# Threshold attention and a three-way maxout FFN on one core: 23 of 288 half tiles masked by GpSimd, two maxout buffers for three, and a new written order

## The chip, the cores and the metric

One core of a Trainium2 chip runs the whole program. The metric is device microseconds of one execution; several executions of a kernel are timed and their median is given. The engines are TensorE (PE in the profile, with PEld for its weight loads), VectorE (DVE), ScalarE (ACT), GpSimd (POOL) and SyncE (SP, which only issues transfers here).

## The reference

Eight batches, eight heads, 576 tokens, head size 64; then a feed-forward block over 4608 tokens with 512 model and 768 hidden columns.

```python
scores = (q @ k.T) / sqrt(64)
scores = where(scores >= rowmax(scores) - tau, scores, -1e9)      # tau = 0.02
attn   = exp(scores - rowmax(scores));  attn /= attn.sum(-1) + 1e-9
x      = concat_heads(attn @ v)                                    # 4608 x 512
out    = maximum(maximum(x @ w1, x @ w2), x @ w3) @ w_out
```

So every score row needs its maximum, a mask (scores more than tau below the maximum count nothing), an exponential, a sum and a division.

## The kernel before, in words

**Tiling.** A tile of scores is 128 query rows by 2 x 576 keys; its two halves (128 x 576, one for each of two heads) are handled apart and are the unit of this text. There are 288 half tiles: 8 batches, 2 groups of four heads in each, 9 row blocks in a group, 2 halves. A half is computed into a PSUM bank pair `sc`; four such bank pairs (numbered 0 to 3) serve all products of TensorE, and each use of one must wait until the use before it has been read out.

**The passes over a half.** `maximum` (DVE) copies the negated scores from PSUM to an SBUF tile `z` (or to one of the two `stage` tiles) and takes their extreme `nm` on the way. After that the digit of the half in the table `MASKED` chooses:

- `0`: `threshold` (DVE, one column) makes `th` = -nm - tau; `exponents` (ACT) masks with a Prelu of slope 2^-100 on one side, and `numerators` (ACT) takes the exponential and the row sum. Two ACT passes, one DVE pass.
- `1`: `exponents` (ACT) takes the exponential; `numerators` (DVE) masks it by comparing with exp(-tau) and sums. One ACT pass, two DVE passes; the second reads `z` twice from SBUF.
- `2` and `3`: like `0` and `1`, but ACT reads the scores from PSUM.

Then `reciprocals` (DVE) gives `rs` for both halves, `normalized` (POOL) writes z times rs as the bf16 tile `P`, and `turned` (SP) issues the transposing transfer from `P` to `ptq`. `product` (TensorE) multiplies values by `ptq` into `o`, which ACT or DVE copies to `xt`.

**The FFN.** For each of six hidden blocks three products `ph` of `xt` with the three weights are formed. ACT copies the first to a tile `hm`, DVE takes the maximum of the second with `hm` in place, and of the third with `hm` into `hT`. Then `po` = hT times the output weights, copied out by ACT as `ob` and stored. The last batch is done in two parts (`SPLIT`).

**The order.** Nothing is scheduled by a program at run time: `ORDER` is a string in which each letter issues one step, and each engine runs its own steps strictly in that order. Capital letters are TensorE's (S scores, T transposes of q and k, O value product, F first half of an FFN product, B its second half, N a ninth chunk), with the bank pair behind most of them. Small letters: m `maximum`, s `threshold`, e `exponents`, k and n `numerators` (k on DVE, n on ACT), r `reciprocals`, p `normalized`, t `turned`, h the ACT copy to `hm`, v the DVE maxima, u the copies `ob`, a and c the copies of transposed q and k, q the swapped copies `qs` (mostly POOL), y and z casts on POOL, l and g loads. All steps are recorded under one line of a helper (L93 in the profile), so the tiles' names tell the groups apart.

Of the kernel before, what the change touches and what calls it, by code (L numbers as in the profile page):

```python
# [21 lines left out]
FLAT = 2.0 ** -100  # L22

MASKED = """
220202110002002100110000100020020312000112012010100000000010100000001100
001000111010000101100000000000110001100000011110110200100000100010000000
110001101110100100010000001001100100000100101111102300000100100000001000
001000110100100001000000000100100001011110100011011100002100001000001013
"""


# [2 lines left out]
ZBUFS = 9  # L34
MORE_Z = 72
PBUFS = 6

SPLIT = {7: ((0, 1), (2, 3, 4))}
# [3 lines left out]
ytS1erkpT2agmnT3pclesqS2aqetS0meqlrnspmS1eqsT2nmpS3tnrcS0zlemS2eprmS3npmtS0npsgS1sermpS2emyS3eptmT0eplmS1ayl  # L42
meS0kynS2tssT3snkynkercperlT3pmnpmntqremS0lasprgeT3pmeS2psstnplnS0mzecesqrmS3etqkeS2gpnmS1npsmtnS0prmleS3pmS
2npsmnS0yrsmetperS2epmO1eqtnkplemnzswT2teS3rplS1empnmS3tpnssrS1klepS0mapermtS2epmT1S3nmqtnkO2qemncpS3txrskT1
peS2rmeS0ptmegpamS2npS1ertsmpnlkzS2elmS3eS0mpnlO1srkepsmnO2tyeprgwnpmT1xS3cpeS0sszmF2eS1meBqkF0ngqT3shrsmBay
S2tvpnF3rpemS1BpemF0pnsvT2BnyctS1esrlsT2mphS3lezS1maF0myntpT2sS3ngrcqF1eBmpnS2svpBnrmS3peS0tmeyF2zmnF3lBsvep
S0rhkBptesF2mgeS1zvF0nsmBpteBsrgvpnF1kS3phS2semBnqmF0S3evqF2ntrmBpelS1spvBnlmS3qhF0rsmepS1tnBpsmS3ezvS2eS1rm
pF0etsyO3mnlkngpO2eswetkBxrmpT3nF2rvpaS1BnqmS0hspS3meF2prS1smntBzesmF3ezvT0tBeclT1yS2pnvS0apsmtS3eyrmlS1epS2
mepF0mnqsmnS3tkBnkeF1restpkumeS2prtBumlperkpS0ustS2umS3pesmS1eqtT0mO2nlpceqsrmO3ntywelkS0pxlS1meF3prnS2smBye
myF0thpskS1oeBpF2nlvF3nlrmBpeBkpS1hstsvS0eF3lrmpnF2mBepBsveF1nT0vBtarkS3lhqS2smleF0prF1mnBysntBveS2plvnS0pom  # L50
F3nyS1pmeBsysmF0thT2rrlpeS1clF3epsmBnqT2svBaS1evqS2nmF0pS3nmqBtnmT2pS1hrcpS3esmS0petF2melS1rmpBnF3skpetF0sve
BlBmnF2vhtF1esrBkpnS0vtT3npBmS2arvpS0ermO3eqtsmepT1swntpS0cF2epesmtnS3kT1nS0mtBessrkpameS3preS1mS0uqmuS3mpnS
1tsmS2pnoS0rempS3lempO1lnkqlemO2lnymeO0srkpetkeF3swxykxpT2BercnprtS1uyS2upmF0termqS3eBymN2lhsskpelkS0eF3ertm
S1pjBlmeS0plvF2npS1mnyF3tpmnBsopT0nvBaS1kF2ieqrssmS0hlpBmelT1qF3snrvF0epcBlepS2vBnpsmtS1nS3rmphS2mnpF1smeS0B
snmF3tevS2T0mF1atBrsekpBevS0thS2pmF3nymS1qeBrsmnpS0tvF2eplF1rmnpBskeBptF3hsvS0eBrsstpmnS1lvT2qeO0mpnlscnT3wS
1etF2srramS0lnqBmlF3eqvT1nBcpS0thF2pemS1perS3mpBnmS0ptesO1smpnkteF3yvxT0BraktyS2esS1vpeS0mpnS3meqF2mnyrmpnT0
S1lceBqmeptrskS0pulS3muS1epmS2teF0rmplnskpeS1mtO3eklekO2esrmpesBknpwxS1kutS2urmopS3nF0myeS1mBetpsmF2hlS3rkep
BlmnF0S1prnsvT3tepBmF2apsssvS1eBtqmeS0qrS3hmtS1epsmF2lnpF0mleF3koBnBrvpeBstyvS1phsS2nmF3emS0nrS1tpmBnprS2smn
F0pveF1pBsremT3ptevBpS2chF0tnmF3ekBT1nvS2aBsmlnF0qvS1eS2rtrespmS3eBmqF1hmpT2nBcpS3ekpT2O0sasvterlmpO2ekqntwS
3xklpS1eF2ssmnF0yrBnmyS3evBptemS1plhS2ssmT3eyF0rcpeF1mBpntT3vnByS2ravpS0nmtpS3nsmS1eF2srmpektepS3slmnS0Bmeqn  # L60
mT1ktuS3urS0lcpeO2rlmpelmpeO3klpelweF1kqnsxS0rkepS2tmS3eBymemepS0kuF3quT2smeBtrF1kphoS0aBmnpS3tsN2rnvplnmpS1
erkpF0tjsF3mnBpsseBvS2ihrS1pmelS0mqeF3S2mnytBpmnoS1rF0eprsvF2ntpmBeBvqF1htskpS3esS0rmetS2pnmF3pBnmF0pesvT2te
BcF1nsBrvpntBskphT2F3erS0vlapBmnF1qvS2etpBmT0hS3rscpnF2lmS1qesS0sempBemS3yF1nvtS0nmBnT2ssrmpO3etspveF0wnS1rk
BpaS3tmhS2elqsF1mlS0qnmS3ermpBF2espsmS0npvBeS3tmeS1rvpO0ntmnsmS2yxS3empF0eskyerT1mpeS2cBtnypsmelkS3ulS2muS1e
smT0O3nsrplnpO2awetmeF3rkpxseT0S1ycntS2meF0poBrnsmpnkpF1ukBurS2shBqemF3oepvS0lS2nsmqF1emBptBnvF0hrrS2speS3mp
F1emBpntT2vepF3BssaktS0nvlBemS2hS1rsmptF0nS3mpeBmtnT2F1svnF3cetBBsrnvpS2hsrqS0meS1pmeT3F2sprmaS0npBmeF3ptsvn
S1qS0mnBtqmeS2yF1prevS0epssBmnS3qmS2htpmF0nlF1keBsmBertvO3pnvepF0serwpT2nBcpF3hktS1eBsrsmpnT0S2vtpaS1remqT3S
0nmyF2qectT1BpasmS3epvS1nS0mqnF2rmpemtpT3eS1keqS0smBercntpS1mupS3emF0ukessS1rmtpnBmopkS2uskS1eO3rukekO0yxeO3
ynwtprmopS0xmpS2emF3peS1mteBrsmpS0nF2pmhtS1nkBS3evF0nstmN2erkpeF1mBjpsBevS2hskF0eF3rkpteBmF1nBpveBkO2hsrvpeS
0rtwS1pnmF2npmS3eBympF1ntrvS0epBmpS2rF3svtpeS0mnpS1sBmiF2smhF0ntkBBervpS1etF3smpnF2BervpS1hsBpnmF0tevS3F1nmB  # L70
etrBkpO2vhO3nspS1xrwepS0mpF3smS2etF1snmBeBstvnS2S0veS3meF1snkeF2rmpnmpeBnkBerrptukpuO3rN1xpuO0jpuO3wptF1xpF2
hF0tvF1vF3hF0vtF1vF2hF0viF1vF2ohF0voF1vF3hF2vF1vF3hF2vO1vO0wF2xF3F1huF0vF3vF2ohF1vF3vF2hF0vF1vF3hF0vF2vF3hF1
vF2vF0hF1vF2vF0uF1ouN0ofjdi
"""


# [28 lines left out]
def kernel(  # L105
# [273 lines left out]
    def exponents(c, r):  # L379
        z = c["z", r]  # L380
        src, sign = (c[r], -1.0) if direct(c, r) else (z, 1.0)
        if masked(c["g"], c["idx"], r):
            scalar.activation(out=z, in_=src, func=AF.Exp, bias=c["nm", r], scale=-sign)
        else:
            th = c["nm", r] if direct(c, r) else c["th", r]
            scalar.activation(out=z, in_=src, func=AF.Prelu, bias=th, scale=sign, alpha=FLAT)

    def numerators(c, r):
        z, acc = c["z", r], c["sm"][:, r:r + 1]
# [89 lines left out]
    def ffn(b, part):  # L479
# [219 lines left out]
    def flow(what, fn):  # L699
        while True:  # L700
# [7 lines left out]
    line = {k: [] for k in "menkrptahvuxwcqsjf"}  # L708
# [10 lines left out]
    def issue(what, where):  # L719
# [27 lines left out]
        elif what == "m":  # L747
            c, r = line["m"].pop(0)
            maximum(c, r)
            line["e"].append((c, r))  # L750
            if not masked(c["g"], c["idx"], r) and not direct(c, r):
                line["s"].append((c, r))
        elif what == "s":
            threshold(*line["s"].pop(0))
        elif what == "e":
            c, r = line["e"].pop(0)
            exponents(c, r)
            line["k" if masked(c["g"], c["idx"], r) else "n"].append((c, r))
        elif what in "nk":
            c, r = line[what].pop(0)  # L760
            if "sm" not in c:
                c["sm"] = small.tile([128, 2], F32, name="sm")
            else:
                c["summed"] = True
            numerators(c, r)
        elif what == "r":
            c = made[line["r"].append(0) or len(line["r"]) - 1]
# [62 lines left out]
```

## Time and profile before

| what | value |
|---|---|
| three runs | 444.09, 441.63 and 441.38 us, median 441.63 |
| span of the profiled execution | 440.2 us (1.43 us below the median of the runs) |
| TensorE, ScalarE, VectorE, GpSimd busy | 95%, 92%, 89%, 72% of the span |
| granted TensorE clock | 0.988 on average |

The profile is that of one execution, taken on the core itself; its span runs from the first to the last instruction, and the timed runs hold what lies around it too. An engine's busy time is the union of its instructions; two neighbouring instructions of one engine overlap a little, so the spacing of starts in the timeline is the price of one in a full queue, and the duration is somewhat more. A busy TensorE is modelled and is not TensorE at its peak.

### The profile page before, as it was taken

The page shows a single profiled execution, that of the slowest core. Times are in us where ns is not written, and L with a number is a line of the kernel's source. Part 1 is how long each engine was busy: PE and PEld are TensorE (multiplying, and loading weights), DVE is VectorE, ACT ScalarE, POOL GpSimd, SP SyncE. Part 2 cuts the span into 40 slices and gives each one's busy share as a digit, 9 for nine tenths or more (in the row PEclk, how much of TensorE's full clock was granted, in tenths as well). Part 3 has the DMA queues.
Part 4 walks back from the last instruction along what each step waited for, and adds up shares of the span by engine and source line. Part 5 has one row for each costly group of instructions (what it writes and reads, how often), then busy time and mean ns, then how long its engine had stood idle before and what let it go on. Part 6 is the DMA issues. An engine that isn't in the chain of part 4 may idle for free.

```text
span 440.2 us, 14283 instructions
## 1 busy us (share of the span) xinstructions
PE 418.9 (95%) x5188; PEld 313.6 (71%) x5190; DVE 393.9 (89%) x1248; ACT 403.6 (92%) x834; POOL 317.0 (72%) x420
## 2 busy tenths in 40 slices
PE   7696789999999999999999999999999999999996
PEld 6353446787788776787678777887688777786873
DVE  4888899999999999999999999999889999998542
ACT  4999999999999999999999999999999998989521
POOL 1988999998787778867786778886585776554400
PEclk9987999999999999999999999999999999999999
DMA  6999999999999999999999999999698778583812
GB/s 190 276 239 214 270 215 260 263 252 252 220 277 224 237 165 242 291 160 232 189 242 238 202 182 273 192 199 208 135 237 153 147 109 185 102 169 72 192 50 85
DMA packets 213959, 88.50 MB, mean 201 GB/s; under 512 B 189184, under 2 KB 202240, under 8 KB 213888
## 3 DMA queue, kind: packets, MB, share of 16 engines
q1 hardware_dynamic: 213360, 86.96, 95.4%
q8 instruction: 41, 0.67, 0.6%
q10 hardware_dynamic: 528, 0.62, 0.5%
q14 instruction: 30, 0.25, 0.2%
HBM read 35.65 MB, written 9.44 MB: 102 GB/s over the span
## 4 chain that ended last, share of the span: by engine, by line
PE 78%; DVE 5%; POOL 5%; issue 4%; ACT 3%; DMA 2%; SPq 1%; DVEq 0%; POOLq 0%; ACTq 0%
PE ph L93 31%; PE sc L93 26%; PE po L93 10%; PE o L93 8%; POOL P L93 4%; PE tp L93 3%; ACT z L93 3%; DVE z L93 3%; DMA qm<-in_q_dram 2%; SPq L93 1%; DVE kt L93 1%; POOL w L93 1%; DVE stage L93 0%; DVE hm L93 0%; POOL qs L93 0%
## 5 line engine op out<-in xcount | busy, mean ns | idle before, releaser
L93 POOL TENSOR_SCALAR P<-z,rs 128x576 bf16<-128x576 f32 x250 | 202.0, 819 | 59.1 <-DVE rs L93 30.4
L93 DVE TENSOR_SCALAR_CACHE_REDUCE z<-sc 128x576 f32<-128x576 f32 x250 | 183.2, 749 | 12.2 <-PE sc L93 8.1
L93 PE MATMUL sc<-kt,qs 64*128 64x256 f32 (+2 forms) x640 | 179.8, 417 | 5.5 <-DVE z L93 3.9
L93 PE MATMUL sc<-kt,qt 64*128 64x320 f32 (+2 forms) x640 | 180.9, 429 | 3.1 <-DVE z L93 1.2
L93 PE MATMUL ph<-xt,w 64*128 64x288 bf16 (+2 forms) x2160 | 172.0, 283 | 0.2 <-DVE hm L93 0.2
L93 PEld LDWEIGHTS <-w 64*128 64x128 bf16 (+1 forms) x2160 | 128.0, 94 | 31.6 <-issue 4.0
L93 ACT ACTIVATE z<-z,th 128x576 f32<-128x576 f32 x161 | 120.5, 767 | 2.2 <-DVE th L93 1.9
L93 ACT ACTIVATE z<-z 128x576 f32<-128x576 f32 x175 | 117.6, 674 | 0.2
L93 PEld LDWEIGHTS sc<-kt,qs 64*128 64x128 f32 (+1 forms) x640 | 92.4, 179 | 22.5 <-DVE z L93 8.6
L93 PEld LDWEIGHTS sc<-kt,qt 64*128 64x128 f32 (+1 forms) x640 | 92.0, 179 | 14.7 <-DVE z L93 3.5
L93 DVE SCALAR_TENSOR_TENSOR z<-z 128x576 f32<-128x576 f32 x75 | 61.7, 827 | 1.4 <-ACT z L93 1.1
L93 POOL COPY qs<-qt 64x640 f32<-64x640 f32 (+3 forms) x66 | 45.9, 695 | 19.5 <-ACT qt L93 16.1
L93 ACT ACTIVATE z<-z,nm 128x576 f32<-128x576 f32 x72 | 53.9, 767 | 0.0
L93 PE MATMUL po<-wo,hT 64*128 64x512 bf16 (+3 forms) x454 | 53.3, 354 | 0.3
L93 DVE TENSOR_TENSOR hm<-ph,hm 128x576 bf16<-128x576 f32 (+2 forms) x54 | 37.0, 685 | 9.8 <-PE ph L93 9.6
L93 ACT ACTIVATE hm<-ph 128x576 bf16<-128x576 f32 (+2 forms) x54 | 31.9, 590 | 14.3 <-PE ph L93 13.8
L93 PEld LDWEIGHTS <-hT 64*128 64x128 bf16 (+2 forms) x456 | 28.4, 95 | 18.5 <-issue 2.6
L93 DVE TENSOR_TENSOR hT<-ph,hm 128x576 bf16<-128x576 f32 (+2 forms) x54 | 36.9, 683 | 2.8 <-PE ph L93 1.0
L93 PE MATMUL o<-ptq,vb 128*64 128x512 bf16 (+2 forms) x544 | 38.7, 282 | 0.2 <-DVE z L93 0.2
L93 POOL TENSOR_SCALAR P<-stage,rs 128x576 bf16<-128x576 f32 x38 | 29.5, 783 | 11.7 <-DVE rs L93 8.4
L93 ACT ACTIVATION_READ_ACCUMULATOR z<-z 128x1 f32 x175 | 33.6, 192 | 0.0
L93 PEld LDWEIGHTS <-vb 128*64 128x64 bf16 x544 | 22.4, 111 | 14.0 <-issue 5.6
(44 smaller groups left out, 412.2 us busy)
## 6 DMA issues: line engine op xcount, KB each, us to landing
vm<-in_v_dram SPq DMA_DIRECT2D x32, 256.0 KB, 4.6
qm<-in_q_dram SPq DMA_DIRECT2D x15, 512.0 KB, 4.7
km<-in_k_dram SPq DMA_DIRECT2D x15, 512.0 KB, 5.4
out_dram<-ob SPq DMA_DIRECT2D x14, 512.0 KB, 4.5
stage<-in_moe_w_dram SPq DMA_DIRECT2D x9, 512.0 KB, 5.6
ptq<-P SPq DMA_TRANSPOSE x144, 4.5
vr<-in_v_dram SPq DMA_DIRECT2D x16, 128.0 KB, 3.8
stage<-in_moe_w_out_dram SPq DMA_DIRECT2D x3, 512.0 KB, 5.5
```

The source lines that it names most:

```text
L93: ins = fn(*a, **kw)
```

## The change

A new digit `4` in `MASKED` stands for 23 half tiles, the 83rd being the first and the 278th the last. For such a half `maximum` and `threshold` run as for `0`. Then GpSimd makes two passes: `marked` (letter b) computes (z + th) times 2^100 and writes it as int8 into the high byte of each element of a bf16 tile `far`, and `moved` (letter C) adds `far` to `z`. `exponents` (letter G) is then a single ACT pass, the exponential with the row sum. There is one `far` tile. The tiles `hm` go from three to two. The digits of other halves change as well: `0` from 187 to 173 halves, `1` from 84 to 78, `2` from 14 to 12, `3` from 3 to 2; the first 48 digits are as before. `ORDER` is a new string almost from its start, with the same steps in it otherwise.

```diff
+    def on_pool(c, r):
+        return by_mask[2 * number[c["g"], c["idx"]] + r] == "4"
     def exponents(c, r):
         z = c["z", r]
         src, sign = (c[r], -1.0) if direct(c, r) else (z, 1.0)
+        if on_pool(c, r):
+            scalar.activation(out=z, in_=z, func=AF.Exp, bias=c["nm", r], scale=-1.0, accum_out=summed(c)[:, r:r + 1])
+            return
...
+    far = [one.tile([128, S], BF16, name=f"far{x}") for x in range(FARS)]
+    for t in far:
+        vector.memset(t, 0.0)
+    def marked(c, r):
+        c["far", r] = t = far[next(fars) % FARS]
+        pool.tensor_scalar(out=t.bitcast(mybir.dt.int8).rearrange("p (n x) -> p n x", x=2)[:, :, 1],
+                           in0=c["z", r], scalar1=c["th", r], scalar2=FAR, op0=OP.add, op1=OP.mult)
+    def moved(c, r):
+        pool.tensor_tensor(out=c["z", r], in0=c["z", r], in1=c["far", r], op=OP.add)
...
-                    st["hm", f] = hp_.tile([128, nr, n], BF16, name="hm", bufs=3)
+                    st["hm", f] = hp_.tile([128, nr, n], BF16, name="hm", bufs=2)
...
-lllllllllT0laqqlcT1aS2lcqqgmS0S3lemS1lmnT2lmeS3lsaS0mnqlqemT3lyerclcapsnS1lS2eqmlS3qemznmS2perS1mnpsmnpT3ske
+llllllllllT0laT1qqlcagS2qqclS0mS3lmS1elmlT2nlmS3elsamS0lqnlT3qmeylrcecapS1snS2qmeS3qmzemnS2peS1rmptT3nsmpnsk
```

Three places show how the steps moved. On ScalarE, the steps ahead of its first copy `hm` (first batch; `z<-z,th` is the Prelu of a half, `z,sm<-z` the exponential with sum, `z<-z,nm` the exponential without). Before:

```order
L93 ACTIVATE xt<-o 128x576
L93 ACTIVATE z<-z,th 128x576 x3
L93 ACTIVATE z,sm<-z 128x576
L93 ACTIVATE hm<-ph 128x576
L93 ACTIVATE qt<-tp 128x2x320
```

and now:

```order
L95 ACTIVATE xt<-o 128x576
L95 ACTIVATE z<-z,th 128x576
L95 ACTIVATE z<-z,nm 128x576
L95 ACTIVATE z,sm<-z 128x576
L95 ACTIVATE hm<-ph 128x576
```

Four softmax passes stood between the last copy `xt` and the first `hm`, now three; over the whole list from the start there are 102 ACT steps ahead of the first `hm` before and 100 now.

On GpSimd, around the 100th of its 288 passes `P` (`vb` and `vr` are casts of values). Before:

```order
L93 TENSOR_SCALAR P<-z,rs 128x576 x8
L93 COPY qs<-qt 64x2x320
L93 TENSOR_SCALAR P<-stage,rs 128x576 x2
L93 TENSOR_SCALAR P<-z,rs 128x576 x3
L93 COPY qs<-qt 64x2x320
```

and now:

```order
L95 CAST vb<-vm 128x1024
L95 TENSOR_SCALAR far_104<-z,th 128x576
L95 TENSOR_SCALAR P<-z,rs 128x576 x3
L95 TENSOR_TENSOR z<-z,far_104 128x576
L95 TENSOR_SCALAR P<-z,rs 128x576
L95 TENSOR_SCALAR P<-stage,rs 128x576
L95 CAST vr_101<-vr 64x128
L95 TENSOR_SCALAR P<-stage,rs 128x576
L95 TENSOR_SCALAR P<-z,rs 128x576
L95 TENSOR_SCALAR far_104<-z,th 128x576
L95 TENSOR_TENSOR z<-z,far_104 128x576
```

The two passes of a half stand among the `P` passes, once with three of them between and once back to back; any `P` behind them waits for them.

On ScalarE, behind a copy `hm` in the third batch. Before:

```order
L93 ACTIVATE hm<-ph 128x576
L93 ACTIVATE z<-z,nm 128x576
L93 ACTIVATE z,sm<-z 128x576 x2
L93 ACTIVATE z<-z,nm 128x576
L93 ACTIVATE hm<-ph 128x576
L93 ACTIVATE z<-z,th 128x576
```

and now:

```order
L95 ACTIVATE hm<-ph 128x576
L95 ACTIVATE z,sm<-z 128x576
L95 ACTIVATE z,sm<-z,nm 128x576
L95 ACTIVATE qt<-tp 128x2x320
L95 ACTIVATE stage<-stage,th 128x576
L95 ACTIVATE stage,sm<-stage,nm 128x576
```

`z,sm<-z,nm` and `stage,sm<-stage,nm` are the single ACT passes of halves with digit `4`; each stands where a half would have had two passes (digit `0`), or one pass and a DVE pass behind it (digit `1`).

More of the change, by code (lines that the diff above doesn't have):

```diff
@@ L24 @@
 MASKED = """
[L25 to L28, printed above, removed]
+220202110002002100110000100020020312000112012010010201000000100100001001
+100010101040100000410440000000010140000400101011001140000001001004000004
+010014001010100100100140000401001040000000101101411014000001400000001400
+010000100101100400400040000001400000101111001110110104000000140111311111
 """
@@ L36 @@
 PBUFS = 6
[L38 removed]
+FARS = 1
+FAR = 2.0 ** 100
+SPLIT = {7: ((0, 1), (2, 3, 4),)}
 ORDER = """
[L41 to L44 removed]
@@ L45 @@
[L45 to L64, printed above, removed]
@@ new lines @@
+ameS0ykyS2nlsT3sskntknrecperlT3pmngpmntqrmS0epsralepmtT3S2epssS0mnpcnzsS3ermS2qgekS1tqemepsnS0pmlS3nprtmS2np
+mepsmS0nyrsnmterS2pepmleO1qtepnkzelmntT2swpeS3rS1epmlnptmS3nssS1rkepS0tmapremS2ptemT1S3qnmnqkO2epmnctS3xrsT1
+kepS2germS0lpempntmapskS0eytS2remS1pemS0pS3nmztT2nsmO1qerclnyO0slwpnkpS1xrmS2eptF0srmepBmnS1lpkF2hgqeBslmS0p
+etrvS1npmS3epF2mtnT0zBsmaS1vyT3esrT2secF0pamBqeS3sknyF2myT1hBplceF0lqsrS3nvtpS1nmBpemS2gqnS3trvpnF1smpBerstS
+0mphS2emzF3nsBsmpgF0evlF1zeBklnS3qgvS2etBrmepF0snsF3pkBhrBmnpS1veF2prmeS0pBvntyS1mhS3ezssF0mtnBmpeS2rvF1tpnS
@@ new lines @@
+3mzeBmgS2npgssO3velketO0emerwpS1xskpF2ntT3mBarkS0phS1semS3qtT2nmF0pncT1lBzarsF2mleS1zvteBeS3pvS0nprmF2nptmep
+kS1elS3ysrmnqtBmeqesS0sprmlF1nlpkeptsS3muBqurmeobkS0luCS2sumS3nT1mpS0GcpO2tnrmpemO1pterssspwS0xsyktS3peF1mnS
+2pmnBtrF0smhpS3esbF1omeBClBnsvS2eF3bmeS0pBvnF2ytmhF1nrBssCT3GvBaS0bvF2ekS3yGF1ymeplBrsF0lpmhBleCBsvteS3vS2np
+rF1mGpS0nmptT3BnrmqF2hsrlsS0pceBlqmT3lS1pasvF0lnqS3mleBptmS2npF1veS3tqmnBpmS0hT2rstS3rnpmF1espsmF0leBpctS3ev
+yS2nsmBbnF1srvF3epBmeptF0khBpeT2vBlCaS1stvS3nrsmO0nplkepS1ewF2ytGrmpnsrsT3mpS0ebtsBcnCnrmS3uS1supmT0GS2pmS3a
@@ new lines @@
+ptmeS1pmS0eS2omqnS3meyS1qrnsO0mpeskpO2etsmxqrsnO3mplewtyeF1knpkT2eBytrrcxpkeqS3uS0umpS2nF1mpteS3myF0esmS2lbe
+BslkCnBlsrN3mhlerpvlespklT1S0jlpS2amtF3pGF1rsmnpBS0sevpS2tnmpBF3hsrmF0pelBpnS1tvS2ynrmBeF3qtveT1BqcS0thymS1p
+nmF2eT3mBlasF0knqS3veS1psrF2srempBtemBpeS3svS1pthmF0nS2smbeS3ssBmnpF1veqtF2rnsBmpBnvpS0hsF3kCteS1mT2nBclyGO0
+rvlpnomepT2S3srwatF1emqS2T0esrpmF3nBpcBnptsvS2eS0bmhF1CnmBS3ervS0qGssmO2pnrmeptF1kepT3BsxS0pvtaS2npmT3S1nlmq
+S0eirbscF2esmCetmBpGsrkpS3urS0umptS1eS2mpeS3spF0mteqmeS1pmnO2kyntsnsmO3erywpnkS1yeS2rpmxBptesrmpeF1kpS2tuS3u
@@ L74 @@
+F1hF0vF3vF1hF2vF0vF3hF1vF0vF3hF1vF0vF3hF1vF0vF2uoN0uoF1jifd
 """
@@ L386, in exponents, with summed @@
             scalar.activation(out=z, in_=src, func=AF.Prelu, bias=th, scale=sign, alpha=FLAT)
+    far = [one.tile([128, S], BF16, name=f"far{x}") for x in range(FARS)]
+    for t in far:
+        vector.memset(t, 0.0)
+    fars = iter(range(1 << 20))
+    def marked(c, r):
[4 more added lines that the diff above has]
+        pool.tensor_tensor(out=c["z", r], in0=c["z", r], in1=c["far", r], op=OP.add)
+    def summed(c):
+        if "sm" in c:
+            c["summed"] = True
+        else:
+            c["sm"] = small.tile([128, 2], F32, name="sm")
+        return c["sm"]
     def numerators(c, r):
-        z, acc = c["z", r], c["sm"][:, r:r + 1]
+        z, acc = c["z", r], summed(c)[:, r:r + 1]
         if masked(c["g"], c["idx"], r):
@@ L707 @@
                 O=products(), F=pieces(), N=iter(lambda: ninths.pop(0), None))
-    line = {k: [] for k in "menkrptahvuxwcqsjf"}
+    line = {k: [] for k in "menkrptahvuxwcqsjfbCG"}
     casts = iter([w[1] for w in wl])
@@ L749, in issue @@
             maximum(c, r)
-            line["e"].append((c, r))
+            if not on_pool(c, r):
+                line["e"].append((c, r))
             if not masked(c["g"], c["idx"], r) and not direct(c, r):
@@ L753, in issue @@
         elif what == "s":
-            threshold(*line["s"].pop(0))
+            c, r = line["s"].pop(0)
+            threshold(c, r)
+            if on_pool(c, r):
+                line["b"].append((c, r))
+        elif what == "G":
+            exponents(*line["G"].pop(0))
+        elif what == "b":
+            c, r = line["b"].pop(0)
+            marked(c, r)
+            line["C"].append((c, r))
+        elif what == "C":
+            c, r = line["C"].pop(0)
+            moved(c, r)
+            line["G"].append((c, r))
         elif what == "e":
@@ L760, in issue @@
             c, r = line[what].pop(0)
[L761 to L764, printed above, removed]
             numerators(c, r)
```

25 lines of the change are left out of this document (16 added, 9 removed).

## The prediction

> **What bounds the kernel now.** I read the page first, its busy times and the shares of the chain that ended last.
>
> ```profile
> PE 418.9 (95%) x5188; PEld 313.6 (71%) x5190; DVE 393.9 (89%) x1248; ACT 403.6 (92%) x834; POOL 317.0 (72%) x420
> PE 78%; DVE 5%; POOL 5%; issue 4%; ACT 3%; DMA 2%; SPq 1%; DVEq 0%; POOLq 0%; ACTq 0%
> ```
>
> TensorE holds most of the chain, but three engines are within 6% of each other, so an average tells little. The next view is the table by stretches, cut where the behaviour changes (time in the stretch, then busy time and count of each engine).
>
> ```profile
> 0.00:80.00 80.00, 63.12 (x616) 40.20 (x618) 65.67 (x222) 72.75 (x153) 65.86 (x92) 0.94 1.08 241
> 100.00:380.00 280.00, 279.60 (x3671) 215.88 (x3668) 269.53 (x855) 275.04 (x562) 211.86 (x279) 1.00 1.02 205
> 380.00:420.00 40.00, 40.00 (x530) 31.05 (x528) 32.39 (x97) 30.66 (x67) 20.25 (x27) 1.00 0.65 138
> 420.00:440.20 20.20, 16.16 (x122) 10.20 (x118) 6.84 (x14) 5.12 (x11) 0.00 (x0) 1.00 0.17 59
> ```
>
> In the first 80 us TensorE idles 16.9 us; ScalarE, after its start, does not: the softmax of the first batch must be through before the first FFN product. From 100 to 380 us all three are nearly full: ScalarE idles 5.0 us of 280, VectorE 10.5, TensorE almost nothing by a busy time that is modelled. GpSimd has 68.1 us free. From 380 on TensorE alone is full, with other engines at 80% or less: there the end is TensorE's own work, then its last copies and stores.
>
> Since TensorE's busy time hides stalls, I take what its weight loads waited for from 100 to 380 us. The view has 23 rows; 18 of them name another engine, of which the first four and the last stand here (total, times, longest).
>
> ```profile
> PEld L93 <- issue: 7.6, 25, 0.4
> ...
> PEld sc L93 <- DVE z L93: 1.4, 5, 0.3
> PEld sc L93 <- ACT z L93: 1.1, 3, 0.4
> ...
> PEld sc L93 <- ACT qt L93: 1.0, 3, 0.5
> PEld tp L93 <- DVE z L93: 0.8, 3, 0.3
> ...
> PEld tp L93 <- ACT ob L93: 0.2, 1, 0.2
> ```
>
> The 18 rows add up to 10.1 us: five on ScalarE (1.1, 1.0, 0.4, 0.4, 0.2) make 3.1, thirteen on VectorE 7.0. That is what faster neighbours can return to TensorE in this stretch; the rest is its own. "PE ph" in the chain is work whose count does not change.
>
> **The change part by part.** *ScalarE.* The digits give the passes: two for `0` and `2`, one for `1`, `3` and `4`. Before, 2 x (187 + 14) + 84 + 3 = 489; now 2 x (173 + 12) + 78 + 2 + 23 = 473, so 16 fewer. Their price in a full queue comes from the timeline (start, duration, instruction).
>
> ```profile
> 203.47 1.43 ACT L93 ACTIVATE z<-z,th 128x576 f32<-128x576 f32 x2
> 204.80 0.67 ACT L93 ACTIVATE z<-z 128x576 f32<-128x576 f32 x1
> 205.38 0.19 ACT L93 ACTIVATION_READ_ACCUMULATOR z<-z 128x1 f32 x1
> 205.47 0.76 ACT L93 ACTIVATE z<-z,nm 128x576 f32<-128x576 f32 x1
> ```
>
> Two Prelu passes fill 203.47 to 204.80, 0.67 each; an exponential with its sum 204.80 to 205.47, again 0.67. So 16 x 0.67 = 10.7 us leave ScalarE, nearly all of it behind the 83rd half.
>
> *VectorE.* `numerators` on VectorE are the halves `1` and `3`: 87 before, 80 now. Thresholds go with `0` and `4`: 187 before, 196 now.
>
> ```profile
> L93 DVE SCALAR_TENSOR_TENSOR z<-z 128x576 f32<-128x576 f32 x75 | 61.7, 827 | 1.4 <-ACT z L93 1.1
> L93 DVE TENSOR_SCALAR th<-nm 128x1 f32<-128x1 f32 x187 | 25.4, 144 | 0.2
> ```
>
> 7 x 0.83 = 5.8 less, 9 x 0.14 = 1.3 more: 4.5 us leave.
>
> *GpSimd* gets 46 passes. `marked` has the shape and the two scalar steps of a `P` pass. `moved` reads two SBUF tensors, which no GpSimd instruction of this trace does. The nearest rows are `P` alone and `P` beside VectorE's pass that reads two SBUF inputs:
>
> ```profile
> L93 POOL TENSOR_SCALAR P<-z,rs 128x576 bf16<-128x576 f32 x250 | 202.0, 819 | 59.1 <-DVE rs L93 30.4
> 202.54 1.47 POOL L93 TENSOR_SCALAR P<-stage,rs 128x576 bf16<-128x576 f32 x2
> 216.95 0.85 DVE L93 SCALAR_TENSOR_TENSOR z<-z 128x576 f32<-128x576 f32 x1
> 217.18 1.24 POOL L93 TENSOR_SCALAR P<-z,rs 128x576 bf16<-128x576 f32 x1
> 321.36 2.61 POOL L93 TENSOR_SCALAR P<-z,rs 128x576 bf16<-128x576 f32 x2
> 322.01 0.75 DVE L93 SCALAR_TENSOR_TENSOR stage<-stage 128x576 f32<-128x576 f32 x1
> 322.69 0.75 DVE L93 SCALAR_TENSOR_TENSOR z<-z 128x576 f32<-128x576 f32 x1
> ```
>
> Alone a `P` takes 0.74 (two in 1.47), beside one such VectorE pass 1.24, beside two of them some 1.9 (2.61 less 0.72): the two engines get in each other's way. I bound each new pass by 0.74 below and 1.24 above, and take 0.74 for `marked`, which reads one tensor as `P` does, and 1.24 for `moved`, which is nearest to the pass that shares its reads. That is 23 x 1.98 = 45.5 us (34 to 57 by the bounds), against the 68.1 free: GpSimd would be 92% busy from 100 to 380 us, from 76%.
>
> The Trainium skill, GPSIMD Engine Reference, section 3.1, has about 2.6 cycles an element at 1.2 GHz for a two-input elementwise pass on GpSimd; for 576 elements an estimate by that page is 1.25 us, and the sum would be the same. No run so far shows it.
>
> *The maxout buffers.* The ACT copy into `hm` must now wait for the third maximum of the block two before it, not three. In the written order at least two full maxima of VectorE stand between that one and the copy, so it is done; VectorE's maxima take 0.75 each and queue ahead. I cost this at nothing; without that cover it would be one maximum, 0.75, for each of the six blocks of a batch.
>
> *The head.* Ahead of the first `hm` ScalarE has 100 steps for 102, at 0.67; ScalarE is the full engine there, so FFN work may begin up to 1.3 us earlier. I take 1.0.
>
> *The sum*, from the span of 440.2: the head, -1.0. TensorE's 3.1 us of waits for ScalarE go, since the relief of 10.7 us is twice what ScalarE idles: -3.1. Of the 7.0 us of waits for VectorE I take 2.0 off, because 4.5 us of relief come back in part when `moved` delays a VectorE pass with two inputs, as the rows at 217 and 322 us show for `P`: -2.0. `P` passes behind the new passes come later, and with them transposes and value products: +1.0 (nothing to +11, below). The end from 380 us is TensorE's and stays. 440.2 - 1.0 - 3.1 - 2.0 + 1.0 = 435.1. The median of the runs is 1.43 above the span, so 436.5 us. A measurement of this kernel tells about 1% from no change: 437.2 and 446.0 are the borders.
>
> **The rivals.** *A, ScalarE alone sets the pace.* Its 5.0 us idle of 280 speak for it, and the relief is the largest term. Then all 10.1 us of waits go and the head's 1.0: 429.1, with the 1.43 some 430.5 us. Against it: VectorE idles only twice as long, and most of TensorE's waits name VectorE.
>
> *B, nothing arrives.* TensorE's real work is the bound, or VectorE is and its relief is eaten by collisions with GpSimd: only the head's 1.0 comes, 439.2 and so 440.6 us. For it: the 100% of TensorE, and its 7.6 us of waits for nothing that another engine does. The mechanism in numbers: VectorE's two-input pass takes 827 ns on average against 0.75 us at 322.01, so it already loses by meeting GpSimd; 23 `moved` passes of 1.24 us that each delay one such pass by half their length cost 14 us, more than the 4.5 won; that needs every one of them to meet, while such passes fill about 80 x 0.8 of VectorE's 394 us, one in six, so some 2.3 us.
>
> The Trainium skill, SBUF — State Buffer, section "Who interferes with whom", states that a VectorE instruction with two SBUF inputs contends with a GpSimd instruction that reads SBUF, and that whichever starts first holds the ports for its whole length. The trace agrees as far as `P` goes (1.24 beside 0.74); by that rule the result of this rival would be the likely one if the new passes met such instructions often.
>
> *C, GpSimd is late, slower.* Every `P` behind a pair of new passes waits for it, and the pass `marked` itself waits for VectorE's `th` in a strict queue. GpSimd's waits show how far ahead it runs today:
>
> ```profile
> POOL P L93 <- DVE rs L93: 28.2, 26, 2.5
> POOL P L93 <- DVE th L93: 3.5, 6, 0.8
> ```
>
> It waits for reciprocals 26 times, 1.1 us each; that is its lead. A pair of 1.98 us is 0.9 more than the lead. The halves `4` lie in twelve groups of four heads, and each group ends with a value product that needs its last `P`. If 0.9 us arrived at each of the twelve ends, that is +10.8: 440.2 - 1.0 - 3.1 + 10.8 = 446.9, with 1.43 some 448.3 us. It decides from the point where a pair costs more than 68.1 / 23 = 2.96 us, or where pairs stand close ahead of a group's end. Against it: no product waits for `ptq` in the trace of before, and the spread of the 46 passes leaves 22.6 us free.
>
> **How the numbers follow.** The forecast has 0.45, with a range of its own from 434 to 440; A 0.10; B 0.25; C 0.20. From the forecast two thirds lie under 437.2, 0.31, and A adds 0.10: faster by over 1% 0.41. Slower: C's 0.18 and 0.03 of B, together 0.21. The rest, 0.38, is within 1%. The range runs from 431.5 to 447: it leaves out half of A and somewhat more than half of C, and takes in the bounds of the two new passes.
>
> **What would show it.** In the profile after, the ACT passes over halves should count 473 and ScalarE's busy time fall by 9 to 11 us; VectorE's `SCALAR_TENSOR_TENSOR` should count 80; GpSimd should be near 362 us, with `z<-z,far` at about 1.24 us and `far<-z,th` at 0.74. ScalarE should idle 10 us or more between 100 and 380 us and TensorE's waits for it be gone. B is right if ScalarE idles and the span stays; C if TensorE waits for `ptq`, or GpSimd's waits for `rs` vanish while `P` comes later. The forecast is wrong if a new pass takes over 1.5 us, if `P` grows well beyond 819 ns, or if the first FFN product does not start earlier.

## The result, and the profile after

The changed kernel takes 457.17 us (median of 4 runs, 456.45 to 457.83), the kernel before, run beside it, 441.95 us (441.38 to 444.09): a ratio of 1.0333, 95% interval 1.0303 to 1.0364. It is 15 us slower. Three executions further on (one of the repaired order without passes, two of the run with GpSimd's loads) ran slower at a lower granted clock, and neither the ratios nor the times given for those two runs hold them. The forecast was 436.5 us with a range from 431.5 to 447; the forecast, its range and all three rivals miss it.

The page after: the span with the count of instructions, the busy times, and the shares of the chain that ended last.

```profile
span 454.7 us, 14268 instructions
PE 427.5 (94%) x5190; PEld 321.3 (71%) x5190; DVE 398.2 (88%) x1244; ACT 397.2 (87%) x825; POOL 363.8 (80%) x466
PE 59%; DVE 10%; POOL 10%; ACT 7%; issue 6%; DMA 5%; SPq 1%; POOLq 0%; DVEq 0%; ACTq 0%
```

TensorE's part of the chain fell from 78% to 59%; GpSimd, VectorE and transfers took its place, though only GpSimd has more to do (363.8 us, forecast 362). The table by stretches says the same:

```profile
100.00:380.00 280.00, 274.46 (x3518) 211.42 (x3516) 258.34 (x810) 264.14 (x551) 247.43 (x313) 1.00 1.00 202
```

In these 280 us TensorE now runs 3518 products where it ran 3671, and every engine but GpSimd idles more than before: ScalarE 15.9 us for 5.0, VectorE 21.7 for 10.5. Faster neighbours gave nothing back; they wait too.

The groups of the new passes on `z` tiles, 16 of the 23 pairs (the other 7 work on `stage` tiles), with P and VectorE's two-input pass (count, busy time, mean ns, idle time before):

```profile
L95 POOL TENSOR_SCALAR far<-z,th 128x576 int8<-128x576 f32 x16 | 13.1, 820 | 1.9 <-DVE th L95 0.5
L95 POOL TENSOR_TENSOR z<-z,far 128x576 f32<-128x576 f32 x16 | 21.2, 1328 | 0.9
L95 POOL TENSOR_SCALAR P<-z,rs 128x576 bf16<-128x576 f32 x250 | 197.0, 802 | 29.5 <-DVE rs L95 9.7
L95 DVE SCALAR_TENSOR_TENSOR z<-z 128x576 f32<-128x576 f32 x70 | 61.3, 882 | 0.2 <-ACT z L95 0.2
```

All 46 new passes together take 50.5 us, forecast 45.5 within 34 to 57. Their sizes are therefore not where the prediction went wrong. That GpSimd's total fits so well is in part luck: the passes P take 4.9 us less than before.

**Where the time goes.** I set the two traces against each other at equal TensorE work (columns streamed since the start). The delay does not grow evenly; it is flat for tens of microseconds and jumps at single places. Worked out from all products of each trace (to some 0.4 us, since a few records are missing), us behind the kernel before at the moment that the kernel before shows on its clock:

| clock of before, us | 75.5 | 97.0 | 118.4 | 161.8 | 204.2 | 289.7 | 331.8 | 374.6 |
|---|---|---|---|---|---|---|---|---|
| after | 0.1 | 3.6 | 4.6 | 6.2 | 8.9 | 11.2 | 13.5 | 14.1 |
| after, no GpSimd passes (below) | -0.2 | 2.7 | 3.5 | 3.4 | 8.9 | 9.3 | 11.4 | 12.4 |
| old order, new masking (below) | 0.0 | 0.0 | 0.9 | 5.6 | 10.0 | 19.1 | 22.6 | 24.2 |

The first marking pass starts at 122.7 us. By then the changed kernel is 4.6 us late, so the passes cannot be the only cause. The chain of waits after names the jumps (start, duration, what the chain goes through):

```profile
72.68 5.28 DMA qm<-in_q_dram
...
87.62 4.88 DMA stage<-in_moe_w_dram
92.56 1.04 POOL w L95
...
169.69 3.11 DMA ptq<-P
172.84 2.63 PE o L95 x20
...
204.19 1.75 POOL stage L95
205.97 0.87 ACT stage L95 x2
...
287.87 1.29 POOL z L95
289.18 2.20 ACT z L95 x5
```

At 78 us the transposition of q waits for a load that SyncE issued at 72.68; at 92.56 GpSimd's weight cast, with everything behind it in GpSimd's strict queue, waits for a load issued at 87.62; at 172.84 a value product waits for a transposing transfer. At 206 and 289 ScalarE's single pass waits for GpSimd's adding pass. So there are two kinds of loss: transfers that the new order issues late, and ScalarE behind GpSimd.

The transfers all go through SyncE's one queue, which the prediction did not read. Its timeline in the kernel before and after, around the transposes that end at the product of 172.84 (start, duration, instruction):

```profile
154.81 6.88 SPq L93 DMA_TRANSPOSE ptq<-P  x3
161.78 0.61 SPq L93 DMA_DIRECT2D out_dram<-ob  x1
```

```profile
161.87 0.53 SPq L95 DMA_DIRECT2D km<-in_k_dram  x1
162.50 1.40 SPq L95 DMA_TRANSPOSE ptq<-P  x1
163.95 0.64 SPq L95 DMA_DIRECT2D vm<-in_v_dram  x1
164.68 6.35 SPq L95 DMA_TRANSPOSE ptq<-P  x3
```

and GpSimd's after:

```profile
165.38 2.91 POOL L95 TENSOR_SCALAR P<-z,rs 128x576 bf16<-128x576 f32 x4
```

The last transpose ahead of that product, the third in the last row of SyncE, turns the tile that the second of these four passes completes, ready at 166.85; SyncE gets to it at 169.69. In the kernel before the same transpose is issued at 160.41, 0.03 us behind its P, and SyncE had been free for 1.9 us (the merged row hides this gap). After the change SyncE has no gap there. Added up over the trace, SyncE issues for 338.8 us of 440 before and 349.9 us after; 144 transposes are 247.9 and 259.0 us of that. Between 40 and 160 us it issues for 18.8 of every 20 us on average, and for 18.5 already before. The full queue itself is therefore not new; what stands in it ahead of which transpose is.

The Trainium skill, Perfetto Trace Analysis, section "What 'DMA-bound' means", lists as one bound of its own that the issuing engine's sequencer shows transfers without a gap. By that rule SyncE's queue should have been read as well. The trace agrees from 40 to 160 us, with 18.8 us of every 20, and the experiment with GpSimd's loads below shows how far it carries.

### The profile page after: what moved, and what is told of

The parts are those of the page before. It is cut to its first block, busy times and chain, and to the rows that moved or that the text cites. A ratio compares the mean times of both kernels' runs of the same rounds, so it can differ in the third digit from the quotient of the medians.

```text
span 454.7 us, 14268 instructions
## 1 busy us (share of the span) xinstructions
PE 427.5 (94%) x5190; PEld 321.3 (71%) x5190; DVE 398.2 (88%) x1244; ACT 397.2 (87%) x825; POOL 363.8 (80%) x466
## 4 chain that ended last, share of the span: by engine, by line
PE 59%; DVE 10%; POOL 10%; ACT 7%; issue 6%; DMA 5%; SPq 1%; POOLq 0%; DVEq 0%; ACTq 0%
PE ph L95 23%; PE sc L95 20%; PE po L95 8%; DVE z L95 6%; PE o L95 5%; ACT z L95 5%; POOL P L95 5%; DMA ptq<-P 2%; PE tp L95 2%; POOL qs L95 2%; SPq L95 1%; DMA qm<-in_q_dram 1%; DMA stage<-in_moe_w_dram 1%; PE warm L95 1%; DVE hm L95 1%
## 5 line engine op out<-in xcount | busy, mean ns | idle before, releaser
L95 POOL TENSOR_SCALAR P<-z,rs 128x576 bf16<-128x576 f32 x250 | 197.0, 802 | 29.5 <-DVE rs L95 9.7
L95 PE MATMUL sc<-kt,qs 64*128 64x256 f32 (+2 forms) x640 | 182.2, 422 | 6.5 <-DVE z L95 4.5
L95 PE MATMUL sc<-kt,qt 64*128 64x320 f32 (+2 forms) x640 | 183.2, 435 | 3.5 <-ACT z L95 1.7
L95 ACT ACTIVATE z<-z,th 128x576 f32<-128x576 f32 x152 | 114.1, 767 | 2.0 <-DVE th L95 1.1
L95 PEld LDWEIGHTS sc<-kt,qs 64*128 64x128 f32 (+1 forms) x640 | 94.3, 181 | 24.2 <-DVE z L95 9.4
L95 ACT ACTIVATE z<-z 128x576 f32<-128x576 f32 x164 | 110.2, 674 | 0.0
L95 PEld LDWEIGHTS sc<-kt,qt 64*128 64x128 f32 (+1 forms) x640 | 94.3, 181 | 16.4 <-DVE z L95 3.5
L95 ACT ACTIVATE z<-z,nm 128x576 f32<-128x576 f32 x84 | 64.0, 768 | 6.2 <-DVE z L95 3.1
L95 PEld LDWEIGHTS <-vb 128*64 128x64 bf16 x544 | 25.1, 111 | 16.2 <-issue 9.7
L95 ACT ACTIVATION_READ_ACCUMULATOR z<-z 128x1 f32 x164 | 31.6, 192 | 0.0
```

The source lines that it names most:

```text
L95: ins = fn(*a, **kw)
```

## The experiments

### What ScalarE's relief is worth

The kernel before, in which 16 halves skip their Prelu, nothing else. These 16 halves go unmasked.

```diff
+            if 2 * number[c["g"], c["idx"]] + r in SKIP:      # 16 halves of digit 0, the 84th to the 276th
+                return                                         # no Prelu; the second pass is a plain exponential
```

> The kernel before with the Prelu pass of 16 halves behind the 82nd left out (these halves stay unmasked): 16 x 0.67 = 10.7 us less on ScalarE, nothing else. The forecast's middle term: TensorE's waits for ScalarE and some more go, 437 to 439 us. The rival, TensorE itself is full from 100 us on: 441 to 442.5 us, and ScalarE idles 10 us more.

Measured: 443.17 us, before 443.04, ratio 1.0015 (0.9976 to 1.0053). Its stretch from 100 to 380 us:

```profile
100.00:380.00 280.00, 279.60 (x3668) 215.91 (x3666) 269.42 (x855) 267.84 (x547) 212.38 (x279) 1.00 1.02 205
```

ScalarE idles 12.2 us instead of 5.0, and TensorE is where it was, 279.60. Even the waits of its weight loads that name ScalarE stay: they add up to 3.6 us, 3.1 before, and the largest row is the same as before.

```profile
PEld sc L94 <- ACT z L94: 1.1, 3, 0.4
```

So taking work from ScalarE returns nothing to the kernel before; the interval leaves no room for the forecast's 3.1 us. No run takes work from VectorE, so that TensorE alone is the bound is argued.

### The passes and the order, apart

The changed kernel without both GpSimd passes (23 halves go unmasked), and without the adding pass alone (their marks are formed and not used):

```diff
-        pool.tensor_scalar(out=t.bitcast(mybir.dt.int8)..., in0=c["z", r], scalar1=c["th", r], ...)   # first run only
-        pool.tensor_tensor(out=c["z", r], in0=c["z", r], in1=c["far", r], op=OP.add)                  # both
+        pass
```

> The changed kernel with both new GpSimd passes left out (23 halves stay unmasked); digits, written order, transfers and everything else as changed. The trace shows 4.6 us of the loss before the first of these passes starts at 122.7 us, and the rest in single steps behind it. Theory 1, the passes make GpSimd late: the rest comes back, 446 to 448 us. Theory 2, the written order places transfers and what needs them too close together, passes or not: 454 to 457 us.

> The changed kernel with the adding pass alone left out (23 halves stay unmasked), the marking pass kept: 23 x 1.28 = 29 us less on GpSimd, 17 to 20 us of new passes stay. Theory 1: between, 449 to 452 us. Theory 2: 454 to 457 us.

Measured: 455.01 us, ratio 1.0267 (1.0230 to 1.0304), and 454.96 us, ratio 1.0274 (1.0233 to 1.0315). Without any of GpSimd's new work the changed kernel is still 12 us slower than before. The order (with the new digits, which take work away) is dear by itself; the passes in it cost 2 to 3 us, and as far as intervals of 1.5 us to either side tell, the adding pass is all of that. What GpSimd waited for from 100 to 400 us, in the kernel before, after, and without the passes (total, times, longest):

```profile
POOL P L93 <- DVE rs L93: 32.6, 29, 2.5
```

```profile
POOL P L95 <- DVE rs L95: 10.1, 10, 4.9
```

```profile
POOL P L95 <- DVE rs L95: 39.4, 27, 4.9
```

The passes do eat GpSimd's lead, 39.4 to 10.1 us, and yet cost little, which fits that the new order has put them where the lead was.

The 12 us are not spread evenly either. In the profiled execution without passes 5.0 of them are one jump, between 164 and 168 us on the clock of before. GpSimd waits there for a transposing transfer to free a tile P, its next P come late, and the value product waits for the transfer of the last one (rows of GpSimd, then of the chain):

```profile
164.00 1.47 POOL L95 TENSOR_SCALAR P<-z,rs 128x576 bf16<-128x576 f32 x2 [2.20 <-DMA ptq<-P]
...
167.44 1.12 POOL P L95 x2
168.56 3.06 DMA ptq<-P
```

With the passes the jump at this place is 1.7 us. The difference of 2 to 3 us between the two runs is therefore a balance of places, not a price per pass.

The opposite test is the passes in the old order. First two passes of the same shapes on a scratch tile, ahead of P of the same 23 halves (all values stay), with two maxout buffers:

```diff
+            if 2 * number[c["g"], c["idx"]] + n in EXTRA:      # the 23 halves
+                pool.tensor_scalar(out=far..., in0=c["z", n], scalar1=c["rs"][:, n:n + 1], ...)
+                pool.tensor_tensor(out=far, in0=c["z", n], in1=far, op=OP.add)
-                    st["hm", f] = hp_.tile([128, nr, n], BF16, name="hm", bufs=3)
+                    st["hm", f] = hp_.tile([128, nr, n], BF16, name="hm", bufs=2)
```

> The kernel before with its own order and digits, and two passes of the same shapes on a scratch tile ahead of the P pass of the same 23 halves, and two maxout buffers for three: GpSimd gets the 46 us of passes and nothing is taken from the other engines. Theory 1: P and the transposes come later, 448 to 453 us. Theory 2: the old order has the slack for them, 442 to 444 us.

Measured: 465.55 us, ratio 1.0514 (1.0479 to 1.0550), far above what was expected. The two parts do not add up: 2 us in one order, 22 in the other. Since these scratch passes stand between a half's reciprocal and its P, I then put the change's own masking into the old order: 23 halves of digit 0, the same or the next, get digit 4. Where two pairs overlap, the one tile of marks holds the marks of the later half, so the mask of two halves is not theirs.

```diff
 the old ORDER, at each of the 23 halves
-s ... e ... n
+sb ... C ... G
```

> The old order with the change's own masking: 23 halves of digit 0, the same ones or the next, get digit 4; GpSimd's first pass is written right behind the half's threshold, its adding pass where ScalarE's first pass stood, the one ScalarE pass where the second stood. Two maxout buffers. ScalarE has 23 passes fewer, 15 us, which by the run with fewer ScalarE passes returns nothing. Theory that the old order has no room for GpSimd's 46 us (its lead of 1.1 us a wait is less than a pair's 2.0, whatever the place): 455 to 467 us, as with the scratch passes (465.55). Rival, that only passes between a half's reciprocal and its P are dear: 443 to 448 us, which would put the whole loss on the new order.

Measured: 467.17 us, ratio 1.0563 (1.0516 to 1.0609). The mechanism is dear in the old order at both places tried, although ScalarE loses 23 passes. The table above shows it at 0.9 us until the first pass and then losing all the way. Its waits from 100 to 400 us:

```profile
ACT z L94 <- POOL z L94: 15.8, 11, 2.9
DVE z L94 <- POOL P L94: 12.3, 19, 1.4
POOL P L94 <- DVE rs L94: 9.5, 10, 2.5
...
ACT stage L94 <- POOL stage L94: 5.5, 3, 3.1
```

and the same of the changed kernel:

```profile
ACT z L95 <- POOL z L95: 2.5, 2, 1.8
ACT stage L95 <- POOL stage L95: 1.7, 2, 1.3
DVE z L95 <- POOL P L95: 3.5, 5, 1.1
```

In the old order ScalarE waits 21.3 us for the adding pass and VectorE's next maximum 12.3 us for a score buffer that a late P still holds (0.6 us in the kernel before); in the new order 4.2 and 3.5 us. So the new order does its work for the passes: it takes their price from 22 or 24 us to 2 or 3, and costs 12 itself. Together that is the 15 us, by the way in which they were split.

### The maxout buffers

The kernel before with two buffers, and the changed kernel with three and without the passes and the tile of marks (23 halves unmasked).

```diff
-                    st["hm", f] = hp_.tile([128, nr, n], BF16, name="hm", bufs=3)
+                    st["hm", f] = hp_.tile([128, nr, n], BF16, name="hm", bufs=2)
```

> The kernel before with two maxout buffers for three, nothing else: all values stay. Prediction on record: the copy into the tile finds the third maximum of two blocks earlier done, so nothing, 441 to 444 us. Rival: the written order of before relies on three buffers, ScalarE's copy waits 0.75 us or more for many of the 54 blocks, and what is behind it on ScalarE with it: 447 us or more; then a part of the 22 us of the old order with the passes (which had two buffers too) is this and not the passes.

> The changed kernel without both GpSimd passes (23 half tiles unmasked), without the tile of marks, and with three maxout buffers: its order and its digits alone. With two buffers it took 455.0 us. If the buffers cost nothing in the new order: 454 to 456. If the third buffer was what kept VectorE and ScalarE apart: under 452.

Measured: 441.82 us, ratio 0.9991 (0.9979 to 1.0002), and 455.68 us, ratio 1.0284 (1.0222 to 1.0347). The buffers cost nothing in the old order, and in the new one nothing that an interval of 2.8 us to either side could show.

### What in the order costs 12 us

Is it the places of the loads? The loads (letters l and g, from the 34th and the 7th on) are put between the same transposes as in the kernel before, in the changed kernel and in the one without passes; and the other way round, the loads l of the new order go into the kernel before. In that last one a transposition of q of the fifth group of heads stands ahead of its load, so a few scores are of older rows.

```diff
 ORDER of the changed kernel, around its 20th transpose
-...germS0lpempntmapskS0eytS2rem...qerclnyO0slwp...
+...germS0pempntlllmapskS0eytggS2rem...qercnyO0swp...
```

> The changed kernel, passes and all, with its loads of q, k, v and of the weights put back between the same transposes as in the kernel before (from the 34th load on); nothing else is moved. In the runs so far SyncE issues transfers 18.9 us of each 20 from 40 to 160 us, and the product that stalls at 171 us waits for a transpose that SyncE issued 2.8 us after its P was ready, with three loads more ahead of it than before. Theory 2a, the place of the loads among the transposes is what makes the new order slow: 445 to 449 us. Theory 2b, the order of the computing engines is: 455 to 459 us.

> As the run with both new GpSimd passes left out (23 halves stay unmasked), with the loads put back between the same transposes as before. Theory 2a: 442 to 445 us, the time before. Theory 2b: 453 to 456 us.

> The kernel before with its loads of q, k and v (not those of the weights) put between the same transposes as in the changed kernel; computing engines as before. Theory 2a: slower, 446 to 453 us. Theory 2b: 441 to 444 us.

Measured: 477.09 us, ratio 1.0756 (1.0723 to 1.0789); 471.73 us, ratio 1.0633 (1.0603 to 1.0662); 453.55 us, ratio 1.0229 (1.0201 to 1.0257). All are slower than the kernels they came from. The third is what theory 2a expected (446 to 453), but the first two contradict it, and the theory that the loads' places are the cause in this simple form falls. SyncE's timeline shows why, in the changed kernel with the old places:

```profile
226.72 6.44 SPq L95 DMA_TRANSPOSE ptq<-P  x3
242.19 0.63 SPq L95 DMA_DIRECT2D vr<-in_v_dram  x1
```

SyncE is idle for 9.0 us ahead of the load of `vr`, until GpSimd's cast has read the tile. A load that comes up before its tile has been read for the last time holds SyncE and every transpose behind it. Six loads of this run wait so, 4.2 to 9.0 us each and 34 us together; in the changed kernel no load waits more than 0.4 us. The granted clock is lower too, 0.90 from 100 to 150 us, and how much of the 20 us that is was not measured. In these three runs the loads' places of one order did not suit the compute steps of the other.

Then the places one by one. Three loads of the changed kernel, its 59th to 61st, move from among transposes 49 to 52 to behind the 54th:

```diff
-...espsmF0leBpctS3evy...khBpeT2vBlCaS1stvS3nrsmO0nplkepS1ew...S3aptmeS1pm...
+...espsmF0eBpctS3evy...khBpeT2vBCaS1stvS3nrsmO0npkepS1ew...S3aptlllmeS1pm...
```

> The changed kernel with only three loads moved: those that stand among its 49th to 51st transpose go behind the 54th, as before. Theory 2a: the stall of 1.7 us at 171 us and the delay right behind it go, 454 to 456 us against 457 us. Theory 2b: no change, 457 us.

Measured: 455.26 us, ratio 1.0273 (1.0244 to 1.0301), 1.9 us under the changed kernel. The wait of 169.69 left the chain; another stands in it further on, of the same kind, and in the profiled execution, the slowest of the four (456.42), it takes back all that was won:

```profile
269.78 5.19 DMA ptq<-P
```

The same with two more repairs, the loads of q and k three transposes earlier (not two, as written below) and the weight load one transpose earlier; and that without the passes (23 halves unmasked):

```diff
-...S0lpempntmapsk...qerclnyO0slwp...S3nvtpS1nmBpemS2gqnS3t...
+...S0lpempnlltmapsk...qercnyO0swp...S3nvgtpS1nmBpemS2qnS3t...
```

> The changed kernel with three repairs of its written order and nothing else: the two loads of q and k that the transposes of q at 78 us wait for are issued two transposes earlier; the weight load that GpSimd's cast waits for at 92.6 us is issued one transpose earlier; the three loads among transposes 48 to 51 stand behind the 54th, as in the kernel before. Theory of single places (each of these transfers is late by itself, and nothing behind it gives the gain back): the losses of 1.6 us at 77, 1.9 at 95 and 1.6 to 1.9 at 171 us go, 457.2 - 5.1 to 5.4 gives 452 us, within 451 to 453.5, and TensorE's gaps over 1.2 us at 76.6, 95.0 and 171 us are missing from the trace. Theory of the matched set (SyncE is full, so whatever is put ahead makes the transposes behind it late): 455 to 459 us, with new gaps of TensorE behind the places.

> The same three repairs, and both new GpSimd passes left out, so 23 half tiles go unmasked. Without the repairs the passes were worth 2.2 us (455.0 against 457.2). Theory of single places: 450 us, within 448.5 to 451.5; what then still lies above 442 us is order that neither the passes nor these places explain. If the passes matter more once TensorE waits less for transfers (they cost 22 us in the old order), it is under 447. Theory of the matched set: 453 to 457.

Measured: 457.61 us, ratio 1.0345 (1.0318 to 1.0372), and 450.69 us, ratio 1.0204 (1.0165 to 1.0243). The first is what the theory of the matched set said, the second what the theory of single places said. With the passes the repairs bring nothing; the chain shows the weight load issued 1 us earlier landing no earlier, and two more of its kind behind it:

```profile
86.62 5.91 DMA stage<-in_moe_w_dram
92.59 1.04 POOL w L95
...
97.39 7.11 DMA stage<-in_moe_w_out_dram
104.56 1.04 POOL wo L95
...
108.64 4.21 DMA stage<-in_moe_w_out_dram
```

Without the passes they bring about 4 us (455.0 to 450.7; by the ratios 0.6%, or 2.8 us, with intervals that just overlap), and the traces show where. At 161.8 us on the clock of before the repaired execution is as late as the one without repairs (3.7 and 3.4 us), so what the two earlier repairs gained is lost by then. At 204.2 it is 4.3 us late for 8.9, and at 374.6 us 8.3 for 12.4: the jump of 5.0 us behind the three loads is gone and does not come back. So, as far as one execution of each tells, the three loads ahead of the transposes were the cause of 4 to 5 of the order's 12 us. With the passes the same repair gained less and was lost further on, and the passes cost 6 us in the repaired order; why they cost more there is not shown.

Last, SyncE's queue itself: the changed kernel without the passes (23 halves unmasked), its weight loads issued by GpSimd.

```diff
-                sync.dma_start(out=my["t"].rearrange("p (k f) -> p k f", k=src.shape[1]), in_=src)
+                pool.dma_start(out=my["t"].rearrange("p (k f) -> p k f", k=src.shape[1]), in_=src)
```

> The changed kernel without both new GpSimd passes (455.0 us; 23 half tiles unmasked), and with the weight loads issued by GpSimd and not by SyncE, at the same places of the text. SyncE is then rid of about 24 x 0.65 = 16 us of issues in the first 130 us, where it runs late. Theory of SyncE's full queue: transposes and the loads of q and k come earlier, the losses at 77, 95 and 171 us shrink, 448 to 452 us. Rival, that the order loses through the engines' own turns: 454 us or more.

Measured: 457.93 us, ratio 1.0347 (1.0254 to 1.0440), from 455.07 and 460.79; the profile is of the lower. The expectation fails as a whole, and its 24 loads were 12, so SyncE was relieved of half of the 16 us named there. Against the kernel before, the profiled execution loses 6.0 us by 75.5 us, where the run without this edit had lost none, and from there to 374.6 us only 6.4 more (6.0 to 12.4) where that one lost 12.6 (-0.2 to 12.4). The start is spoiled; behind it half of the order's loss is gone, most of it at 164 to 168 us, where this execution loses about 1 us for 5.0. That fits a full SyncE as half of the cause, but one execution of a run that spreads so far does not show it.

### By which chain a late GpSimd pass arrives

The waits of the old order point at score buffers. Four runs have ten of them for nine, and five P buffers for six to make room: the kernel before, the old order with scratch passes, the changed kernel, and the changed kernel with three repairs.

```diff
-ZBUFS = 9
+ZBUFS = 10
-PBUFS = 6
+PBUFS = 5
```

> The kernel before with ten score buffers for nine and five P buffers for six; all values stay. It is the control of the next three. Theory of score buffers (GpSimd's late P hold the buffers that VectorE's next maximum needs): VectorE waits only 3.0 us for P in the kernel before, so it stays within 439 to 444 us. Theory of P buffers (a P is held until SyncE has got to its transpose, up to 6 to 10 us late): one buffer less makes GpSimd wait for transposes, 446 us or more.

> The old order with the two extra GpSimd passes ahead of 23 P passes (465.55 us with nine score buffers), now with ten score buffers and five P buffers. Theory of score buffers: VectorE's waits for P fall from 15.8 us (z and stage) to under 8, and the time to 452 to 459 us. Rival, the passes reach TensorE by late P, late transposes and late value products: nothing is gained, 463 us or more.

> The changed kernel with ten score buffers and five P buffers. Theory of score buffers: the passes' 2.2 us and part of the order's losses go, 452 to 455 us, and VectorE's waits for P (6.6 us) fall by half. Rival, the new order's losses are waits for transfers only: 456 to 459 us, the gaps at 77, 95, 171 and 327 us stay.

> The changed kernel with the three repairs of its order (457.61 us) and ten score buffers, five P buffers. In the repaired order the passes cost 6 us and VectorE waited 10.2 us for P. Theory of score buffers: most of these 6 us come back, 451 to 454 us. Rival, transfers: 456 to 460 us.

Measured: 445.57 us, ratio 1.0076 (1.0052 to 1.0101); 464.39, 1.0501 (1.0451 to 1.0551); 456.55, 1.0332 (1.0313 to 1.0351); 458.37, 1.0411 (1.0346 to 1.0475). No run came down to what the theory of score buffers expected, and where the passes are, each lies in the range of its rival. VectorE's waits in the old order with passes fell (13.5 to 5.2 us on z, while those on stage rose from 2.3 to 5.3), but the control shows the price of the buffer that was taken, GpSimd waiting for transposes to free a P:

```profile
POOL P L93 <- DMA ptq<-P: 10.0, 4, 5.5
DVE z L93 <- POOL P L93: 3.2, 7, 1.5
```

The control lost 0.8% by this, some 3.4 us, and a gain of that size from the tenth score buffer would not be seen in the other runs. So this edit cannot separate the two chains. That score buffers alone carry the delay is not borne out.

## Why the prediction was wrong, point by point

- **The bound.** I took the first reading, TensorE holds 78% of the chain, and then let 10.1 us of its waits for other engines count as returnable. Rival B was nearer to the truth: nothing arrives. The run with 16 passes fewer measured it: 0.1 us for the forecast's 3.1, with 3.6 us of such waits left. In the changed kernel the weight loads' waits for ScalarE did not go either: they sum to 2.8 us for 3.1, the largest now "PEld sc" for a copy `hm`:

```profile
PEld sc L95 <- ACT hm L95: 1.3, 3, 0.9
```

- **VectorE's term of 2.0 us** had no run of its own; VectorE idles 11 us more from 100 to 380 us, and nothing in the time shows that any of it arrived.
- **The head, 1.0 us.** Two passes fewer ahead of the first `hm` did not start the FFN earlier: its first product begins at 71.46 us, before at 71.32.
- **The moved steps, costed at nothing.** This step failed most. Of a new order I counted only what stood ahead of one copy and behind some P passes, and the sum has no term for the rest and no reason for leaving it out. SyncE's queue, full for 18.5 of 20 us from 40 to 160 us already before, and the loads' and transposes' places in it were not read at all. The order without the passes measured 12 us.
- **P later, 1.0 us (nothing to 11).** In the new order the passes cost 2 to 3 us, inside the bounds, which is partly luck, since it is a balance of places; in the old one 22 and 24, twice the upper bound. The 68.1 us of free time were the wrong row: free time in the mean was no room at the places where the passes stood. The lead of 1.1 us a wait was nearer.
- **Rival C** had the sign, and 448.3 us for what became 457.2. Its price came from value products that wait for `ptq`. The jump at 172.84 is one, yet the run without passes has it too; in the old order the passes arrive by ScalarE's wait for the adding pass, a link that C did not hold. Its point of decision, a pair of 2.96 us, was wrong: pairs of 2.2 us (50.5 / 23) were enough.
- **Right:** the durations of both passes (0.74 and 1.24 forecast; medians 0.75 and 1.28, the second above its bound), 473 ScalarE passes, 80 two-input passes of VectorE, the maxout buffers, and, partly by luck, GpSimd's 362 us. ScalarE's busy time fell by 6.4 us, not by 9 to 11: seven more passes write a sum, whose read-out of 0.19 us was left out, and neighbouring instructions overlap 2.5 us less where ScalarE idles. In the chances two thirds of 0.45 are 0.30, not 0.31.

The Trainium skill, GPSIMD Engine Reference, section 3.1, gave 1.25 us as an estimate for the adding pass. The trace agrees, 1.28 in the median.

The Trainium skill, SBUF — State Buffer, section "Who interferes with whom", has VectorE's two-input pass and GpSimd's reading passes hold each other up. The trace agrees: in the kernel before that pass takes 0.75 us wherever no GpSimd pass overlaps it, and 0.85 us on average beside one. Its mean on `z` tiles went from 827 to 882 ns, and to 865 in the run without the new passes, so most of the 55 ns is not theirs.

**Still open:** the greater part of the order's 12 us. Its largest jump, 5 us without the passes, is shown to come from three loads ahead of the transposes, by the run that moved them (with two other repairs). The jumps at 78 and 92.56 us are late transfers by their rows, but issuing these earlier gained nothing that lasted. That SyncE's full queue is the common cause is argued and only half supported. A run with GpSimd's loads behind the start alone was not tried.

## What to carry to other kernels

Where an order is written by hand, price a new order as a change of its own: read the queue that issues transfers as an engine, with its full stretches, before costing any moved step at nothing. An engine's mean free time was no room for new work here: 50 us of passes in 68 us of free time cost 22 us or more in one order and 2 to 3 in another. Read its lead at those places, and what waits behind it in a strict queue (here ScalarE's behind GpSimd's). Before counting waits for a neighbour as gains, take that neighbour's work away in one run: here it returned nothing.

## What the runs showed of the hardware

A transpose's issue holds SyncE 1.43 us in the median, before and after. In the mean of one run it is 1.36 to 1.51 us with no plain load or store issued in the 6 us before it, and 2.3 to 2.8 us with four or more (the kernel before, the changed one, and four runs of the new order); I had taken issuing as free. Whether the loads are the reason was not tested. Twelve weight loads issued by GpSimd in place of SyncE landed in about the same time (medians 5.5 us for 5.3, and 6.4 for 5.6), and yet the profiled execution was 6.0 us behind by 75.5 us.
